# Value products of a fused attention and gated-convolution kernel: two 64-row halves abreast instead of whole 128-row products

## The chip, the cores and the metric

The kernel runs on one core of one Trainium2 chip, in one launch. The metric is the device time of that launch in microseconds, the median of several runs. Beside the times there is one profiled execution, whose trace gives the start and length of every instruction.

## The reference

Eight batches are computed. In each, twelve heads attend over 448 positions with 64 values per head, with a softmax that has one more term in its denominator; the result, 448 x 768, goes through a gated long convolution that is computed by a Fourier transform along the sequence.

```python
scores = scale * np.matmul(q, k.transpose(0, 1, 3, 2))
m = np.max(scores, axis=-1, keepdims=True)
e = np.exp(scores - m)
attn = e / (np.sum(e, axis=-1, keepdims=True) + np.exp(-m) + 1e-09)
...
proj = x @ w_proj
x1, x2, x3 = (proj[..., :D].copy(), proj[..., D:2 * D].copy(), proj[..., 2 * D:].copy())
X2 = np.fft.rfft(x2, n=S, axis=1)
H = np.fft.rfft(filter_fft, n=S, axis=0)[None, :, :]
x2_conv = np.fft.irfft(X2 * H, n=S, axis=1)
y = x1 * x2_conv * x3
return (y @ w_out).astype(np.float32)
```

The change touches only the last product of the attention, `attn @ v`.

## The kernel before

**Attention, pair by pair.** Two heads are worked on together, so there are 8 x 6 = 48 pairs, numbered by `i`. The 448 keys of a head are three blocks of 128 and a remainder of 64. The two remainders of a pair share one block of 128: this is block 0, blocks 1 to 3 are the heads' own keys. `attention(i)` (L859) makes these tasks:

- `scores(t)` (L866): for block 0 one matmul over 128 rows (L873). For blocks 1 to 3 two matmuls (L871), one per head, each over 64 rows (a head has 64 values): head 0 lies on rows 0 to 63 of the array, head 1 on rows 64 to 127, and each writes its own PSUM bank. The two run abreast.
- `exps(t)` (L875): ScalarE's exponentials, from PSUM into the tile `e` (or `er` for block 0), keys on partitions, 448 queries of each head along the row.
- `out_rests` (L898, matmul at L902): the value product of the two remainders. Eight matmuls of 64 rows, 65 columns wide (64 values and a column of ones, which sums the denominator), head 0 on rows 0 to 63, head 1 on rows 64 to 127, each into its head's own bank. The first one of a head opens its sum (`start=True`).
- `out_rest(u)` (L907, matmul at L910): the value product of the own keys of head `u`. Twelve matmuls: four blocks of 128 queries by three blocks of 128 keys, each over all 128 rows, all into head `u`'s bank. There are two such tasks per pair, 96 in all; the text calls them the first and the second value task.
- `norm` (L918): VectorE divides by the denominator once both value tasks are done.

**Dense part.** `dense(b)` (L1027) does projection, transform, gate and output of batch b: matmuls over 128, 113 or 112 rows, 384 to 456 columns wide (L1083, L1105, L1154, L1206, L1253, L1019). A batch's dense part is mixed with the attention of later batches. Near the start, gaps of TensorE that the plan foresees are filled with matmuls on a zero tile (L1501).

**What sets the order.** The kernel is a list of tasks (`add`, L83): engine, cost, what a task needs and makes, what it takes and gives back, and for TensorE the `rows` of the array that it uses (128 unless it is said). `Plan.run` (L92) goes through them at build time and writes out each engine's instructions in a fixed order; with `plan.ORDER` given (L435) an engine's tasks stand in the order of the numbers in that tuple, one number per task, 2135 of them. The plan reckons 0.093 us (`SWITCH`, L66) each time that TensorE's `rows` change from one task to the next. On the chip every engine takes its instructions in that order and waits on semaphores.

**SyncE** (SP) issues nearly all DMAs: loads of q, k and v (L496, L501, L662, L683, L513, L648), transposes by DMA of q, k, of the attention's result and of the transform's input (L632, L639, L977, L1122), and stores (L1339, L1342): 250 in this run. An issue takes SP's time, a transposing one more, and an issue whose data or room is not ready holds up everything behind it. GpSimd converts the loaded q, k and v to bfloat16.

The lines that the change replaces:

```python
def out_rest(u):
    for n in range(NST):
        for t in (0, 2, 1):
            nc.tensor.matmul(
                out_bank(u)[:, n, :],
                P["e"][1 + t][:, u * S + n * 128 : u * S + n * 128 + 128],
                vn[b % 2][:, hp, 4 * u + t, :],
                start=False, stop=(n == NST - 1 and t == 1),
            )
```

Of the kernel before, what the change touches and what calls it, by code (L numbers as in the profile page):

```python
# [18 lines left out]
B, H, S, DH = 8, 12, 448, 64  # L19
D = H * DH  # L20
SP = 112
NST = S // SP
NDT = D // 128
NHP = H // 2
# [17 lines left out]
class Plan:  # L42
# [40 lines left out]
    def add(self, eng, cost, want, emit, need=(), make=(), take=(), give=(), dma=0.0, run=256, n=1, after=0.0, begun=(), late=0.0, turn=False, part=None, keep=False, port=False, rows=128):  # L83
        want = self.ORDER[len(self.tasks)] if self.ORDER else want + self.SHIFT.get(part, 0.0)
        if eng == "SP":
            dma *= self.STRETCH
        if eng == "DVE" and port:
            cost += self.SHARED
        cost, dma, run, late = self.TIMES.get(len(self.tasks), (cost, dma, run, late))
        self.tasks.append((want, len(self.tasks), eng, cost, emit, need, make, take, give, dma, after, run, n, begun, late, turn, keep, port or eng == "POOL" and not dma, rows))  # L90
# [227 lines left out]
def kernel(  # L318
# [11 lines left out]
    nc = tc.nc  # L330
# [69 lines left out]
    vn = [const.tile([128, NHP, 7, DH + 1], BF16, name=f"vn{i}") for i in range(2)]  # L400
# [22 lines left out]
    def stage(g, at, n):  # L423
# [4 lines left out]
    plan = Plan(  # L428
        {
            "e": 6, "er": 2, "e3": 3, "er3": 1, "k0": 2, "q0": 2, "u": 1, "w": 1, "xf": 1,  # L430
            "x2": 1, "x2s": 1, "x2b": 2, "xs": 2, "t0": 2, "t1": 2, "yh": 1, "g": 1, "x1": 2, "cr": 2, "cw": 1, "cv": 2, "yT": 1, "yR": 1,
            "os": 3,
        }
    )
# [3 lines left out]
    add = plan.add  # L438
# [23 lines left out]
    def tau(i, frac=0.0):  # L462

        if i >= NHP * n_batches:
            return tau(i - 1, frac + 1)
        h = i % NHP + frac
        return ATT[i // NHP] + SLOT[i // NHP] * min(h, 3) + LATER[i // NHP] * max(h - 3, 0)
# [391 lines left out]
    def attention(i):  # L859
# [15 lines left out]
        def exps(t):  # L875
            if t:
                P["e"][t] = e = third[t] if i in THIRD else es[(3 * turn_of(i) + t - 1) % 6]
                to, of = e[:, 0 : 2 * S], pair(("sc", ("S", i, t)))[:, :, 0:S]
                if b < NSTAGED:
                    to = to.rearrange("p (u n) -> p u n", u=2)  # L880
                else:
                    to = to.rearrange("p (u n j) -> p u n j", u=2, j=NST)
                    of = of.rearrange("p u (j n) -> p u n j", j=NST)
                nc.scalar.activation(to, of, AF.Exp, scale=SCALE)  # L884
            else:
                P["e"][t] = e = third[0] if i in THIRD else er[turn_of(i) % 2]
                to, of = e[:, 0:S], bank(("hy", ("S", i, t)))[:, 0:S]
                if b >= NSTAGED:
                    to, of = to.rearrange("p (n j) -> p n j", j=NST), of.rearrange("p (j n) -> p n j", j=NST)
                nc.scalar.activation(to, of, AF.Exp, scale=SCALE)  # L890

        def out_banks():
            return pair(("op", i))[:, :, 0 : NST * (DH + 1)].rearrange("p u (n d) -> p u n d", n=NST)

        def out_bank(u):
            return out_banks()[:, u]

        def out_rests():  # L898
            for n in range(NST):
                for u in range(2):  # L900
                    c = slice(64 * u, 64 * u + 64)
                    nc.tensor.matmul(  # L902
                        out_bank(u)[:, n, :], P["e"][0][c, n * 128 : n * 128 + 128], vn[b % 2][c, hp, 3, :],
# [3 lines left out]
        def out_rest(u):  # L907
            for n in range(NST):
                for t in (0, 2, 1):
                    nc.tensor.matmul(  # L910
                        out_bank(u)[:, n, :],
                        P["e"][1 + t][:, u * S + n * 128 : u * S + n * 128 + 128],
                        vn[b % 2][:, hp, 4 * u + t, :],
                        start=False,
                        stop=(n == NST - 1 and t == 1),
                    )
# [41 lines left out]
        for u in range(2):  # L958
            add("PE", 0.37, w + 0.01 * u, lambda u=u: out_rest(u), need=[("ER", i)], make=[("V", i, u)],
                take=[("op", i)], give=[(third_of[0], (i, t)) for t in range(1, 4)])  # L960
# [521 lines left out]
    with (  # L1482
        tc.tile_pool(name="tabs", bufs=1) as tp,
        tc.manual_schedule(engines={E.PE, E.Pool, E.DVE, E.Activation, E.SP}),
    ):
        zero1 = tp.tile([128, 1], F32, name="zero1")
        warm = tp.tile([128, 1], F32, name="warm")
        add("DVE", 0.1, -20.0, lambda: nc.vector.memset(zero1, 0.0), make=["zero1"])
        add("POOL", 0.36, -20.0, count, make=["count"])
        add("POOL", 0.51, -19.0, lambda: make_identity(nc, ident_bf), make=["ident"])  # L1490
        first = tp.tile([1, 16], BF16, name="first")
        add("POOL", 0.64, -18.5, lambda: nc.gpsimd.dma_start(first, moe_w_out[0:1, 0:16]), need=["ident"], dma=0.05)
        add("DVE", 0.2, -19.5, number, need=["count"], make=["row"])
        add("DVE", 2.3, -19.0, phases, need=["row"], make=["phases"])

        idle = tp.tile([128, 128], BF16, name="idle")
        add("DVE", 0.15, -19.9, lambda: nc.vector.memset(idle, 0.0), make=["idle"])

        def fill(i, count):
            for _ in range(count):  # L1500
                nc.tensor.matmul(psum[:, 512 * i : 512 * i + 128], idle, idle)  # L1501

        plan.fill = fill

        def spin():

            t = bank(("hy", "spin"))
            for _ in range(SPIN):
                nc.tensor.matmul(t[:, 0:128], idle, idle)

        add("PE", 3.65, -20.0, spin, need=["idle"], make=["spin"], take=[("hy", "spin")], give=[("hy", "spin")])
        add("ACT", 0.8, -18.0, lambda: nc.scalar.copy(ks, idle[:, None, :].to_broadcast([128, NHP, 128])), need=["idle"], make=["zero ks"])

        add("ACT", 1.3, -20.0, lambda: nc.scalar.activation(warm, zero1, AF.Sin), need=["zero1"], make=["sine table"])
        add("ACT", 0.6, -19.0, sines, need=["phases", "sine table"], make=["sines"])
        add("ACT", 1.5, -16.0, lambda: nc.scalar.activation(warm, zero1, AF.Exp), need=["zero1", "sines"], make=["exp table"])

        def pads():
            for e in es:
                nc.gpsimd.memset(e[:, 2 * S :], 0.0)  # L1520
            for e in er:
                nc.gpsimd.memset(e[:, S:], 0.0)
            nc.gpsimd.memset(third[3][:, 2 * S :], 0.0)

        add("POOL", 0.8, 7.0, pads, make=["pads"], after=6.5)

        def ones(i):
            nc.gpsimd.memset(vn[i][:, :, :, DH : DH + 1], 1.0)
        for i in range(2):
            add("POOL", 0.08, (6.0, 24.0)[i], lambda i=i: ones(i), make=[("ones", i)],  # L1530
                after=(6.5, 16.0)[i])
        for b in range(n_batches):
            if b < NSTAGED:
                staged(b)
            else:
                loaded(b)
        add("DVE", 0.5, tau(NHP * NSTAGED) - 30.0, lambda: nc.vector.memset(kn[:, :, 0, :], 0.0),
            need=[("c" + x, g) for x in "kqv" for g in range(NHP * NSTAGED - NHP, NHP * NSTAGED - 2)], make=["zero kn"])
        for (part, ch), at in zip(LOADS, LOAD):
            if part == "F":  # L1540
                add("POOL", 1.79, at, filter_load, need=["ft", "bps"], make=["filt"], take=[("yT", "F")], dma=3.6, run=115, n=3, late=0.76, after=at)
            elif part == "O":
                add("POOL", 0.82, at, wout_load, make=["wout"], need=[("V", THIRD[-1], 0), ("V", THIRD[-1], 1)], dma=5.95, run=115, late=-0.34, after=at)
            elif ch is None:
                add("POOL", 0.82, at, lambda part=part: wproj_load(part, None), make=[("w", part, 0), ("w", part, 1)], dma=4.9,
                    run=115, late=-0.34, after=at)
            else:
                add("POOL", 0.82, at, lambda part=part, ch=ch: wproj_load(part, ch), make=[("w", part, ch)], dma=2.95, run=55, late=-0.34 if ch else 1.2, after=at)
        more_tables()
        filter_spectrum()  # L1550
        for i in range(n_batches * NHP):
            attention(i)
        for b in range(n_batches):
            dense(b)
        watch()
        tc.mark_branch_hint_location("overflow", 0, engines=[E.PE, E.DVE])
        plan.run()
# [55 lines left out]
```

## Time and profile before

| | |
|---|---|
| time, median of 3 runs | 368.22 us (367.34 to 368.5) |
| profiled execution, first to last instruction | 365.4 us |
| TensorE busy | 358.2 us, 3628 matmuls |
| VectorE, ScalarE, GpSimd busy | 261.7, 263.4, 114.0 us |
| granted TensorE clock | 1.000 throughout |
| DMA | 69.20 MB, mean 189 GB/s |

The profiled execution's span is 2.8 us shorter than the median time; what lies around the span is not in the trace. In the rows below, a group of instructions is shown with its line, engine, operation, what it writes and reads, the shape of the weights and of the moving data, its count, its busy time and the mean length of one. A matmul's length is from its start to its modelled end, so that lengths overlap; the pace is read from the starts. PEld is the weight load that goes with each matmul. SPq is SyncE's queue.

### The profile page before, as it was taken

What the parts mean: (1) busy time and instruction counts of PE and PEld (TensorE: products, weight loads), DVE (VectorE), ACT (ScalarE), POOL (GpSimd) and SP (SyncE); (2) the same over time, 40 slices, a digit from 0 to 9 for tenths busy, and PEclk for the clock granted to TensorE, in tenths of its full rate; (3) what the DMA queues carried; (4) which work ended last, traced back from release to release, by engine and by line L of the source; (5) the groups of instructions that cost most, each with busy time, mean ns of one, the idle gap of its engine ahead of it and who ended that gap; (6) DMA issues with size and microseconds to landing.
All of it is one profiled execution on the core that took longest, in us unless ns stands there. A gap on an engine that the chain in (4) does not pass through costs nothing. (4 is left out here: it accounts for less than half of the span.)

```text
span 365.4 us, 9379 instructions
## 1 busy us (share of the span) xinstructions
PE 358.2 (98%) x3628; PEld 213.2 (58%) x3629; DVE 261.7 (72%) x671; ACT 263.4 (72%) x453; POOL 114.0 (31%) x247
## 2 busy tenths in 40 slices
PE   7999999999999999999999999999999999999995
PEld 6777665656664555655565555654555556555653
DVE  5669299877899549785777758893677867759570
ACT  6989777778796668875777667888877885465433
POOL 7872363315333454345324442700110000000000
PEclk9999999999999999999999999999999999999999
DMA  8999989999999999999999999999942165035025
GB/s 204 270 253 240 248 170 230 230 207 216 157 251 268 249 225 247 200 268 229 260 215 224 309 206 210 210 226 189 219 108 43 45 88 131 0 88 130 26 110 175
DMA packets 135299, 69.20 MB, mean 189 GB/s; under 512 B 91917, under 2 KB 131664, under 8 KB 135248
## 3 DMA queue, kind: packets, MB, share of 16 engines
q1 hardware_dynamic: 130528, 62.90, 78.4%
q0 software_dynamic: 4480, 5.41, 8.8%
q8 instruction: 29, 0.48, 0.6%
q10 hardware_dynamic: 240, 0.23, 0.2%
q14 instruction: 22, 0.18, 0.2%
HBM read 43.86 MB, written 11.01 MB: 150 GB/s over the span
## 5 line engine op out<-in xcount | busy, mean ns | idle before, releaser
L884 ACT ACTIVATE e<-psum 128x896 bf16<-128x896 f32 x138 | 123.0, 922 | 28.8 <-PE psum L871 23.7
L1206 PE MATMUL psum<-xT,wproj_bf 128*128 128x448 bf16 x576 | 121.7, 352 | 0.2 <-DMA xT<-xb 0.2
L1206 PEld LDWEIGHTS <-wproj_bf 128*128 128x128 bf16 x576 | 53.9, 98 | 46.6 <-issue 3.4
L1019 PE MATMUL psum<-wout_bf,yT 128*128 128x384 bf16 (+2 forms) x287 | 54.1, 326 | 0.2
L1105 PE MATMUL psum<-xf,wproj_bf 128*128 128x456 bf16 x216 | 45.7, 356 | 0.0
L910 PE MATMUL psum<-vn,e 128*128 128x65 bf16 x1104 | 45.1, 194 | 0.0
L910 PEld LDWEIGHTS <-e 128*128 128x128 bf16 x1104 | 39.8, 98 | 8.9 <-issue 4.5
L871 PE MATMUL psum<-qT,kT 64*128 64x448 bf16 x288 | 41.9, 354 | 0.2 <-DMA kT<-nat 0.2
L1172 DVE TENSOR_TENSOR t<-xs,hrs 113x768 bf16<-113x768 bf16 (+1 forms) x64 | 39.1, 631 | 3.0 <-ACT xs L1166 2.8
L1222 DVE TENSOR_TENSOR g<-x,psum 128x448 bf16<-128x448 bf16 x42 | 26.0, 618 | 19.0 <-PE psum L1206 16.2
L1332 ACT COPY osb<-psum 128x384 f32<-128x384 f32 (+2 forms) x56 | 26.0, 485 | 17.7 <-PE psum L1019 13.1
L668 POOL CAST nat<-nat 112x512 bf16<-112x512 f32 x36 | 24.3, 679 | 44.1 <-DMA nat<-in_q_dram 44.1
L1166 ACT CAST xs<-psum 113x384 bf16<-113x384 f32 (+1 forms) x64 | 29.1, 484 | 12.3 <-PE psum L1154 8.4
L1019 PEld LDWEIGHTS <-yT 128*128 128x128 bf16 x288 | 27.1, 98 | 18.5 <-issue 1.2
L925 DVE TENSOR_TENSOR xb<-psum,den 128x512 bf16<-128x512 f32 x48 | 33.2, 691 | 1.7
L1220 ACT CAST x<-psum 128x448 bf16<-128x448 f32 x42 | 22.4, 539 | 13.3 <-PE psum L1206 11.7
L700 POOL CAST vn<-nat 128x192 bf16<-128x192 f32 x58 | 21.7, 406 | 32.9 <-DMA nat<-in_v_dram 31.0
L1262 ACT CAST cr<-psum 128x452 bf16<-128x452 f32 x48 | 24.5, 544 | 10.1 <-PE psum L1253 9.2
L1105 PEld LDWEIGHTS <-wproj_bf 128*128 128x128 bf16 x216 | 20.1, 98 | 19.7 <-issue 2.4
L890 ACT ACTIVATE er<-psum 128x448 bf16<-128x448 f32 x46 | 25.4, 555 | 6.9 <-PE psum L873 6.2
L688 POOL CAST nat<-nat 128x384 bf16<-128x384 f32 x29 | 17.6, 612 | 26.6 <-DMA nat<-in_k_dram 24.7
L923 DVE TENSOR_SCALAR den<-psum 128x8 f32<-128x8 f32 x48 | 7.9, 164 | 23.9 <-PE psum L910 23.3
(138 smaller groups left out, 482.0 us busy)
## 6 DMA issues: line engine op xcount, KB each, us to landing
nat<-in_q_dram SPq DMA_DIRECT2D x47, 224.0 KB, 4.6
out_dram<-osb SPq DMA_DIRECT2D x23, 384.0 KB, 3.7
nat<-in_k_dram SPq DMA_DIRECT2D x41, 192.0 KB, 4.7
nat<-in_v_dram SPq DMA_DIRECT2D x41, 192.0 KB, 3.9
wproj_bf<-in_moe_w_proj_dram POOLq DMA_DIRECT2D x2, 1152.0 KB, 12.7
rests<-in_k_dram SPq DMA_DIRECT2D x8, 192.0 KB, 5.0
rests<-in_v_dram SPq DMA_DIRECT2D x8, 192.0 KB, 4.7
out_dram<-osb SPq DMA_DIRECT2D x8, 192.0 KB, 3.2
```

Of the source, the lines that this page charges most:

```text
L871: nc.tensor.matmul(sc[:, u, 0:S], kT[b % 2][c, hp, t, :], qT[b % 2][c, hp, :])
L884: nc.scalar.activation(to, of, AF.Exp, scale=SCALE)
L890: nc.scalar.activation(to, of, AF.Exp, scale=SCALE)
L910: nc.tensor.matmul(out_bank(u)[:, n, :], P["e"][1 + t][:, u * S + n * 128 : u * S + n * 128 + 128], vn[b % 2][:, hp, 4 * u + t, :], start= ...
L925: nc.vector.tensor_tensor(W["xb", b][:, hp].rearrange("p n (u d) -> p u n d", u=2), op[:, :, :, 0:DH], rec[:].unsqueeze(3).to_broadcast([1 ...
L1019: nc.tensor.matmul(ops[:n, : c.stop - c.start], y[:, dt, 0:n], wout_bf[:, dt, c], start=(dt == 0), stop=(dt == NDT - 1),)
L1105: nc.tensor.matmul(pps, wproj_bf[:, kt, D + dt * 128 : D + (dt + 1) * 128], W["xf", b][:, kt], start=(kt == 0), stop=(kt == NDT - 1),)
L1166: nc.scalar.copy(L["xs", par, ch][:K, pg % 2, :], L["Z", pg, ch][:K, :DCH])
L1172: nc.vector.tensor_tensor(t[:K], L["xs", par, ch][:K], h, op=ALU.mult)
L1206: nc.tensor.matmul(p[:, :S], wproj_bf[:, kt, 2 * part * D + dt * 128 : 2 * part * D + (dt + 1) * 128], xT()[:, kt, 0:S], start=(kt == 0), ...
L1222: nc.vector.tensor_tensor(g[:, dt, :], L["x1", dt], p[:, :S], op=ALU.mult)
L1332: (nc.vector.tensor_copy if half else nc.scalar.copy)(L["os", st][:n, c.start + lo : c.start + hi], L["O", st, ch][:n, lo:hi])
```

## The change

A value task no longer belongs to one head. Both tasks of a pair work on both heads, with matmuls of 64 rows: the first task (`s = 0`) multiplies the first 64 keys of each block of head 0 (rows 0 to 63) and the last 64 keys of each block of head 1 (rows 64 to 127), alternating; the second (`s = 1`) the halves that are left, crosswise: head 1 on rows 0 to 63, head 0 on rows 64 to 127. So within a task each head's bank is written from one half of the rows, and between the tasks the two banks change hands. A task has 24 matmuls where it had 12.

Between the two tasks stands a no-operation on SyncE: it waits for the last matmul of the first task, and the first matmul of the second task waits for it. In the list of tasks it is a task of SP of its own, which needs `("va", i)` from the first value task and makes `("vb", i)` for the second; there are 48. Costs: 0.38 for a value task (0.37 before), 0.18 for the no-operation; both value tasks are now marked `rows=64`. `plan.ORDER` is another tuple, with 48 numbers more; `plan.TIMES` is as before.

```diff
-    plan.ORDER = (3, 0, 1, 124, 1, 2, 0, 0, 1, 2, 3, 4, 2, 4, 18, 0, ...)
+    plan.ORDER = (2, 0, 4, 52, 3, 4, 0, 0, 2, 1, 3, 4, 2, 1, 5, 0, ...)
...
+        def follow(ins, other):
+            if other is not None:
+                tc.add_manual_dep(
+                    ins.ins,
+                    other.ins.name,
+                    mybir.DependencyInfo(mybir.DependencyClass.Sync, mybir.DependencyReason.DATA),
+                    reason="the rows of two banks change hands",
+                )
...
-        def out_rest(u):
+        def out_rest(s):
             for n in range(NST):
                 for t in (0, 2, 1):
-                    nc.tensor.matmul(
-                        out_bank(u)[:, n, :],
-                        P["e"][1 + t][:, u * S + n * 128 : u * S + n * 128 + 128],
-                        vn[b % 2][:, hp, 4 * u + t, :],
-                        start=False,
-                        stop=(n == NST - 1 and t == 1),
-                    )
+                    for half in range(2):
+                        u, c = half ^ s, slice(64 * half, 64 * half + 64)
+                        ins = nc.tensor.matmul(
+                            out_bank(u)[:, n, :],
+                            P["e"][1 + t][c, u * S + n * 128 : u * S + n * 128 + 128],
+                            vn[b % 2][c, hp, 4 * u + t, :],
+                            start=False,
+                            stop=(s == 1 and n == NST - 1 and t == 1),
+                        )
+                        if not (n or t or half):
+                            follow(ins, P["swap"] if s else None)
+            if not s:
+                P["swap"] = ins
+
+        def swap():
+            ins = nc.sync.nop()
+            follow(ins, P["swap"])
+            P["swap"] = ins
+
+        P["hand over"] = swap
...
         for u in range(2):
-            add("PE", 0.37, w + 0.01 * u, lambda u=u: out_rest(u), need=[("ER", i)], make=[("V", i, u)],
-                take=[("op", i)], give=[(third_of[0], (i, t)) for t in range(1, 4)])
+            add("PE", 0.38, w + 0.01 * u, lambda u=u: out_rest(u), need=[("vb", i) if u else ("ER", i)], make=[("V", i, u)] + ([] if u else [("va", i)]),
+                take=[("op", i)], give=[(third_of[0], (i, t)) for t in range(1, 4)], rows=64)
...
+        for i in range(n_batches * NHP):
+            add("SP", 0.18, tau(i + 1), T[i]["hand over"], need=[("va", i)], make=[("vb", i)])
```

2 lines of the change are left out of this document (1 added, 1 removed).

## The prediction

> **What bounds the kernel.** I read the page first, then the busy time by stretches, then the order of time on TensorE and on SyncE, then the end of the chain of waits. From the page, the span and TensorE with its clock:
>
> ```profile
> span 365.4 us, 9379 instructions
> PE 358.2 (98%) x3628; PEld 213.2 (58%) x3629; DVE 261.7 (72%) x671; ACT 263.4 (72%) x453; POOL 114.0 (31%) x247
> PEclk9999999999999999999999999999999999999999
> ```
>
> The stretches (columns: busy us and count of PE, PEld, DVE, ACT, POOL; granted clock; share of the DMA engines; GB/s), and the matmuls that fill foreseen gaps:
>
> ```profile
> 5.00:46.00 41.00, 39.59 (x541) 27.72 (x539) 24.99 (x71) 34.01 (x56) 23.45 (x50) 1.00 1.14 254
> 46.00:106.00 60.00, 59.51 (x670) 37.91 (x667) 52.70 (x124) 46.90 (x78) 26.52 (x55) 1.00 1.05 205
> 165.00:265.00 100.00, 99.83 (x980) 55.98 (x979) 70.34 (x177) 74.74 (x130) 34.51 (x68) 1.00 1.09 227
> 265.00:310.00 45.00, 45.00 (x489) 26.14 (x488) 32.82 (x92) 33.26 (x56) 1.75 (x4) 1.00 0.39 82
> ```
>
> ```profile
> L1501 PE MATMUL psum<-idle x101: 217/219/294, 4.7 to 35.0; 128*128 128x128 bf16 x101
> ```
>
> From 46 to 310 us TensorE has work all the time, at full clock; nobody else comes near. So there the time is the sum of TensorE's paces, and what shortens it shortens the kernel. Up to 35 us it is otherwise: 101 filling matmuls stand where TensorE waits for loads. The DMA engines are loaded (share at or over 1) until 265 us.
>
> A busy row hides what a matmul costs; the starts show it (start us, us until the last one's end, what, count):
>
> ```profile
> 13.88 0.90 PE L910 MATMUL psum<-vn,e 128*128 128x65 bf16 x24
> ...
> 45.66 0.91 PE L910 MATMUL psum<-vn,e 128*128 128x65 bf16 x24
> ...
> 199.77 1.30 PE L1206 MATMUL psum<-xT,wproj_bf 128*128 128x448 bf16 x6
> 201.00 0.30 PE L902 MATMUL psum<-vn,er 64*128 64x65 bf16 x8
> 201.13 0.55 PE L871 MATMUL psum<-qT,kT 64*128 64x448 bf16 x4
> 201.61 1.31 PE L1206 MATMUL psum<-xT,wproj_bf 128*128 128x448 bf16 x6
> 202.76 0.53 PE L910 MATMUL psum<-vn,e 128*128 128x65 bf16 x12
> 203.12 2.47 PE L1105 MATMUL psum<-xf,wproj_bf 128*128 128x456 bf16 x12
> 205.43 0.35 PE L873 MATMUL psum<-qT,kT 128*128 128x448 bf16 x1
> ...
> 207.24 0.74 PE L871 MATMUL psum<-qT,kT 64*128 64x448 bf16 x6
> 207.91 2.48 PE L1105 MATMUL psum<-xf,wproj_bf 128*128 128x456 bf16 x12
> 210.33 0.30 PE L902 MATMUL psum<-vn,er 64*128 64x65 bf16 x8
> 210.46 0.35 PE L871 MATMUL psum<-qT,kT 64*128 64x448 bf16 x2
> 210.75 0.91 PE L910 MATMUL psum<-vn,e 128*128 128x65 bf16 x24
> ...
> 301.43 0.54 PE L910 MATMUL psum<-vn,e 128*128 128x65 bf16 x12
> ```
>
> Six L1206 matmuls take 1.15 us to the next start when a 128-row product follows (201.61 to 202.76) and 1.23 when a 64-row one does (199.77 to 201.00). Twelve L1105 take 2.31 before a 128-row product and 2.42 before a 64-row one. Two, four and six scores of 64 rows take 0.29, 0.48 and 0.67 until a 128-row product starts: 0.19 per abreast pair and 0.10 besides. So each change between 64 and 128 rows costs 0.08, 0.11 and 0.10: 0.097 us on the mean.
>
> **Changes of rows: the gain.** I sorted TensorE's 712 tasks by the numbers of the old and of the new tuple, with the rows that each task names, and counted neighbours whose rows differ: 164 before, 124 after. The new tuple gathers a pair into blocks such as remainder product, scores, first value task, two scores, second value task, all of 64 rows. With the old tuple and new rows it would be 222: the order, not the halving, makes the gain. Up to the last pair's second value task 41 are saved (one comes back at the end): 15 up to that of pair 6 (the row at 45.66), 26 after it. 26 x 0.097 = 2.5 us, on TensorE's path, where nothing covers it. The 15 early ones, 1.5 us, lie where TensorE waits for loads; they are worth from 0, if all becomes waiting, to 1.5. I take half, 0.7.
>
> **The value matmuls themselves.** Twice as many, half as high:
>
> ```profile
> L910 PE MATMUL psum<-vn,e 128*128 128x65 bf16 x1104 | 45.1, 194 | 0.0
> L902 PE MATMUL psum<-vn,er 64*128 64x65 bf16 x368 | 13.3, 191 | 0.1
> ```
>
> The new form is that of L902 at three times the length. L902's 368 stand in 46 groups of eight, 13.3 / 46 = 0.289 us each; less the last one's own 0.191, four pairs start within 0.098, so a pair takes about 0.031. Twelve whole products last 0.53 (202.76), less 0.194, over eleven steps: 0.0305 each. A task of twelve pairs against twelve whole ones thus costs 0 to 0.01 us more, 96 tasks 0 to 1.0; I take 0.5. No row shows 24 in one run; a shortage of weight loads or of issue would show there, and is a rival below. The sentence of the Trainium skill that speaks against this part is on its page "TensorE: Matmul & The Clock Gate", section "Wait — 56ns, not 53.3ns?": matmuls never start less than about 25 ns apart, however narrow; 24 in a task would then take an estimated 0.60 us, and the 96 tasks some 22 us more than now. The trace disagrees where 64-row halves alternate: eight in 0.13 us (201.00 to 201.13), 16 ns apart.
>
> **The hop over SyncE.** It goes: last matmul of the first task ends, the no-operation wakes and ends, TensorE's second task wakes. The nearest rows are at the end of the chain of waits, and SP's own short instruction at L639:
>
> ```profile
> 356.60 0.04 issue
> 356.64 3.73 PE psum L1019 x21
> ...
> 360.43 1.26 PE psum L1019 x8
> 361.69 0.04 DVEq L1332
> 361.73 0.04 issue
> 361.77 0.30 DVE osb L1332
> ```
>
> ```profile
> L639 SPq DMA_TRANSPOSE kT<-nat x16: 1188/1860/3036, 60.7 to 245.2; - x16
> L639 SPq EVENT_SEMAPHORE  x12: 17/17/282, 60.6 to 233.0; - x12
> ```
>
> 0.19 for the matmul to end, 0.08 from its end into a waiting engine by way of its sequencer (361.69 to 361.77), 0.04 onto TensorE (356.60): 0.31 and the no-operation. Under it lie, by the new tuple, in 33 of 48 pairs exactly two scores of 64 rows, 0.38 to 0.39 us, and the 0.03 until they start: 0.42. The no-operation may take 0.11. I take the semaphore instruction's 17 ns, as it also only waits, so a hop to an idle SP is free; the other end is a DMA issue (0.47 at 203.31 below), 0.36 over, in 48 pairs 17 us. Eight pairs have more work between, four early ones one score only (about 0.1 late each, in the filled stage), three others about as much as the 33.
>
> That holds if SP is already waiting in the no-operation. In the trace of before it mostly would not be:
>
> ```profile
> 13.52 2.21 SPq L496 DMA_DIRECT2D nat<-in_q_dram  x1
> ...
> 203.31 0.47 SPq L683 DMA_DIRECT2D nat<-in_v_dram  x1
> ...
> 301.40 1.28 SPq L1122 DMA_TRANSPOSE x<-nat  x1
> ```
>
> Taking the end of each pair's first value task as the hop's moment, SP is inside a DMA issue at 35 of 48, with 24.1 us left in all, 0.69 each; the first is pair 0, whose twelve matmuls from 13.88 on are done at 14.4, with SP busy until 15.7, the last pair 46, from 301.43 and done at 302.0, with SP busy until 302.7. The new order puts the no-operations between the issues, so that SP should stand ready: it must then finish what is ahead in time. Ahead of 14 no-operations is a transposing DMA (1.19 to 3.04 us at L639), of 5 a store that needs a result copied first, of 4 another no-operation, of 25 a load. A late one holds TensorE, which cannot pass its second value task: 0.69 less the 0.09 that is left of the cover, 0.60 us each. I take one, 0.6 us; both ends are under the rivals. Behind a waiting no-operation stand the next loads, transposes and stores; GpSimd's conversions wait for those, then the scores. Loads lie well ahead of their use in the steady part, so I price this at nothing there; without that lead it is a rival.
>
> **Elsewhere.** VectorE's division still follows the second value task. 1152 more matmuls and loads cost only the pace counted above. The new tuple moves other tasks too; TensorE's idle time to be had or lost outside the changes is small in the stretches above (0.49 us of 60, 0.17 of 100), and I put it at 0.
>
> **Sum.** -2.5 - 0.7 + 0.5 + 0.6 = -2.1 us: span 363.3 for 365.4. The median stands 2.8 us over the span, and I let that stay: 368.2 - 2.1 = 366.1.
>
> **Rivals.**
>
> *The hops give the gain back* (no change). Without a late hop the sum is -2.7. Three to six late ones leave -0.9 to +0.9: 367.3 to 369.1. For it: an SP that would be busy at 35 of 48 moments, and transposes of scattered length. Against: between two hops SP has some 6 us and about five issues (250 issues, 48 pairs in 290 us), and a wait for TensorE sets it right again. Loads held behind waiting no-operations, with the DMA engines at a share over 1, would do the same.
>
> *SyncE's issues become the bound* (slower). The same wait, at seven hops or more: from +1.5 us on. In the part up to 265 us a transpose that takes 3.0 us instead of 1.2 makes every later no-operation late until SP catches up. Seven to fourteen late hops give 369.7 to 373.9; all 35 would be +18, 386. Against: SP may stand waiting most of the time.
>
> *Halves don't run abreast when 24 follow each other* (slower). If each takes a whole product's 0.0305, a task takes 0.73 for 0.37, 96 tasks +35 us: 403. Eight at 16 ns speak against it. (The page's floor of 25 ns, above, is the milder form, some +22 by the estimate there.)
>
> *The early changes* are inside the forecast: early changes worth 0 and two late hops give -2.5 + 0.5 + 1.2 = -0.8, about 367.4; all worth 1.5, no dearer matmuls and no late hop -4.0, 364.2.
>
> **How the numbers follow.** Forecast 0.52 (364.2 to 367.1, as far as it is faster), gain given back 0.23, SyncE the bound 0.23, halves in turn 0.02. A measurement here tells 0.3%, 1.1 us, from no change. The range goes from 364.2 up to nine late hops, -2.7 + 5.4, rounded to 371.0; left out are the upper part of SyncE's case, 0.12, halves in turn, and a little below. Faster 0.52, same 0.23, slower 0.25.
>
> **What would show it.** The value matmuls as 2304 of 64x65, with about 0.37 us from the start of a task to the next start; about 40 fewer steps of 0.097. If 0.4 us or less lies between first and second value task, the hop is free; a second task starting after an idle TensorE, with SP's no-operation starting late behind a DMA issue, is the second or third case. A no-operation over 0.11 us with SP idle before it, or a task of over 0.45 us, would prove me wrong; so would filling matmuls or early idle time that grow by what the early changes save.

## The result, and the profile after

The changed kernel takes 384.85 us, the median of 4 runs (380.91 to 386.59); the kernel before took 368.05 us (4 runs, 367.34 to 368.5). The ratio is 1.0435, with a 95% interval of 1.0376 to 1.0494: slower, where 366.1 us and at most 371.0 had been forecast. The profiled execution is the fastest of the four, 380.91 us with a span of 379.0; the last section says what that hides. In the experiments below, two executions (389.08 and 386.61 us) fell in a slower state of the chip and do not count in the ratios; without them the medians of their kernels are 382.35 and 381.33 us.

The page of after: the span, the engines, and TensorE's clock in 40 slices.

```profile
span 379.0 us, 11681 instructions
PE 357.4 (94%) x4744; PEld 216.8 (57%) x4745; DVE 254.2 (67%) x671; ACT 262.4 (69%) x452; POOL 108.8 (29%) x247
PEclk9999998999999999999999999999999999999999
```

TensorE is busy for 0.8 us less than before, and the span is 13.6 us longer. It stands idle instead. Where it does is seen in the stretches that the prediction shows of before, and in 106 to 165 us, whose row of before follows (busy us and count of PE, PEld, DVE, ACT, POOL; granted clock; share of the DMA engines; GB/s):

```profile
5.00:46.00 41.00, 37.41 (x630) 25.99 (x629) 25.19 (x72) 33.85 (x55) 21.89 (x47) 1.00 1.15 241
46.00:106.00 60.00, 54.58 (x851) 35.95 (x851) 42.22 (x110) 41.00 (x69) 21.48 (x48) 0.97 0.99 193
106.00:165.00 59.00, 56.78 (x756) 31.80 (x754) 39.28 (x99) 43.34 (x75) 24.02 (x53) 1.00 1.04 231
165.00:265.00 100.00, 98.04 (x1313) 56.92 (x1312) 71.96 (x186) 73.44 (x126) 32.97 (x70) 1.00 0.98 222
265.00:310.00 45.00, 44.79 (x686) 26.76 (x685) 30.90 (x83) 36.83 (x62) 4.47 (x9) 1.00 0.47 99
```

Before, from 106 to 165 us:

```profile
106.00:165.00 59.00, 58.84 (x604) 32.30 (x602) 44.69 (x111) 44.95 (x77) 23.85 (x51) 1.00 1.12 245
```

From 46 to 106 us TensorE idles for 5.42 us (0.49 before), from 106 to 165 for 2.22 (0.16 before), from 165 to 265 for 1.96 (0.17 before), and from 5 to 46 for 3.59 (1.41 before). From 265 us on, where the share of the DMA engines is down at 0.47, it idles for 0.21 us of 45.

The groups of TensorE's matmuls, with what ended the idle time before them (busy us, mean ns of one | idle us before and releaser):

```profile
L1041 PE MATMUL psum<-wout_bf,yT 128*128 128x384 bf16 (+2 forms) x287 | 54.3, 326 | 2.6 <-ACTq L1585 1.9 <-ACT osb L1354 0.6
L921 PE MATMUL psum<-vn,e 64*128 64x65 bf16 x2208 | 49.3, 191 | 7.7 <-SPq L934 7.6
L911 PE MATMUL psum<-vn,er 64*128 64x65 bf16 x368 | 13.3, 191 | 1.9 <-POOL vn L556 1.7 <-ACT e L884 0.2
```

L921 is the value matmul and L934 the no-operation. Read by itself this points at the hop, 7.6 us of it, in 9 waits. That reading turns out to be wrong as an answer to where the time went, and the experiments below are about it.

The steady part looks as foretold. The order of time on TensorE (start us, us until the last one's end, what, count):

```profile
208.53 0.28 PE L911 MATMUL psum<-vn,er 64*128 64x65 bf16 x8
208.65 0.53 PE L921 MATMUL psum<-vn,e 64*128 64x65 bf16 x24
209.02 0.54 PE L871 MATMUL psum<-qT,kT 64*128 64x448 bf16 x4
209.40 0.53 PE L921 MATMUL psum<-vn,e 64*128 64x65 bf16 x24
209.86 1.31 PE L1228 MATMUL psum<-xT,wproj_bf 128*128 128x448 bf16 x6
```

24 halves take 0.37 us until the scores start, the second task follows 0.38 us later behind two pairs of scores, and the hop costs nothing. The no-operation is a semaphore instruction of 17 ns:

```profile
L934 SPq EVENT_SEMAPHORE  x48: 17/17/17, 12.5 to 315.8; - x48
```

It goes otherwise at 57 us. SyncE's and TensorE's order of time there:

```profile
50.93 0.63 SPq L501 DMA_DIRECT2D nat<-in_v_dram  x1
59.78 0.98 SPq L683 DMA_DIRECT2D nat<-in_k_dram  x2
```

```profile
57.16 0.53 PE L921 MATMUL psum<-vn,e 64*128 64x65 bf16 x24
60.26 0.95 PE L921 MATMUL psum<-vn,e 64*128 64x65 bf16 x30 [2.56 <-SPq L934]
```

The load of v issued at 50.93 lands at 59.0; SyncE stands until then at the next load, which waits for it, and the no-operation of the waiting pair comes after that, at 60.2. TensorE idles for 2.56 us. Of the 48 no-operations 16 start more than 0.15 us after their first value task is done, 1.2 us on the mean; 12 of them lie between 57 and 200 us, where the share of the DMA engines is about 1.

### The profile page after: what moved, and what is told of

It reads as the page before. It is cut to its first block, busy times and chain, and to the rows that moved or that the text cites. A ratio compares the mean times of both kernels' runs of the same rounds, so it can differ in the third digit from the quotient of the medians.

```text
span 379.0 us, 11681 instructions
## 1 busy us (share of the span) xinstructions
PE 357.4 (94%) x4744; PEld 216.8 (57%) x4745; DVE 254.2 (67%) x671; ACT 262.4 (69%) x452; POOL 108.8 (29%) x247
## 5 line engine op out<-in xcount | busy, mean ns | idle before, releaser
L884 ACT ACTIVATE e<-psum 128x896 bf16<-128x896 f32 x138 | 121.3, 922 | 23.2 <-PE psum L871 19.3
L1228 PEld LDWEIGHTS <-wproj_bf 128*128 128x128 bf16 x576 | 54.8, 98 | 48.1 <-issue 3.2
L1041 PE MATMUL psum<-wout_bf,yT 128*128 128x384 bf16 (+2 forms) x287 | 54.3, 326 | 2.6 <-ACTq L1585 1.9
L921 PE MATMUL psum<-vn,e 64*128 64x65 bf16 x2208 | 49.3, 191 | 7.7 <-SPq L934 7.6
L921 PEld LDWEIGHTS <-e 64*128 64x128 bf16 x2208 | 41.8, 95 | 17.3 <-SPq L934 15.0
L871 PE MATMUL psum<-qT,kT 64*128 64x448 bf16 x288 | 42.9, 352 | 1.2 <-DMA qT<-nat 0.4
L1194 DVE TENSOR_TENSOR t<-xs,hrs 113x768 bf16<-113x768 bf16 (+1 forms) x64 | 36.8, 592 | 7.2 <-ACT xs L1188 7.1
L1041 PEld LDWEIGHTS <-yT 128*128 128x128 bf16 x288 | 27.0, 98 | 21.1 <-issue 3.2
L668 POOL CAST nat<-nat 112x512 bf16<-112x512 f32 x36 | 23.4, 654 | 43.9 <-DMA nat<-in_q_dram 42.7
L1242 ACT CAST x<-psum 128x448 bf16<-128x448 f32 x42 | 22.6, 543 | 15.1 <-PE psum L1228 14.9
L1127 PEld LDWEIGHTS <-wproj_bf 128*128 128x128 bf16 x216 | 20.5, 98 | 18.5 <-issue 0.4
L688 POOL CAST nat<-nat 128x384 bf16<-128x384 f32 x29 | 15.1, 530 | 30.0 <-DMA nat<-in_k_dram 29.9
## 6 DMA issues: line engine op xcount, KB each, us to landing
wproj_bf<-in_moe_w_proj_dram POOLq DMA_DIRECT2D x2, 1152.0 KB, 11.5
```

The source lines that it names most:

```text
L871: nc.tensor.matmul(sc[:, u, 0:S], kT[b % 2][c, hp, t, :], qT[b % 2][c, hp, :])
L921: ins = nc.tensor.matmul(out_bank(u)[:, n, :], P["e"][1 + t][c, u * S + n * 128 : u * S + n * 128 + 128], vn[b % 2][c, hp, 4 * u + t, :], ...
L1041: nc.tensor.matmul(ops[:n, : c.stop - c.start], y[:, dt, 0:n], wout_bf[:, dt, c], start=(dt == 0), stop=(dt == NDT - 1),)
L1127: nc.tensor.matmul(pps, wproj_bf[:, kt, D + dt * 128 : D + (dt + 1) * 128], W["xf", b][:, kt], start=(kt == 0), stop=(kt == NDT - 1),)
L1194: nc.vector.tensor_tensor(t[:K], L["xs", par, ch][:K], h, op=ALU.mult)
L1228: nc.tensor.matmul(p[:, :S], wproj_bf[:, kt, 2 * part * D + dt * 128 : 2 * part * D + (dt + 1) * 128], xT()[:, kt, 0:S], start=(kt == 0), ...
```

## The experiments

Each run is compared with the kernel before on the same chip; in brackets stands the 95% interval of the ratio. The theories of the first four runs: **A**, the hop over SyncE and SyncE's late no-operations are the cause (as the third case of the prediction has it); **B**, the newly laid order is slow by itself, with or without crossing; **C**, 24 halves cost more than 12 whole products.

**The new order without crossing.** The halves stay on their rows (head 0 on 0 to 63, head 1 on 64 to 127) in both tasks, and the no-operation goes; half of the keys are counted twice and the other half left out.

```diff
-                        u, c = half ^ s, slice(64 * half, 64 * half + 64)
+                        u, c = half, slice(64 * half, 64 * half + 64)
...
-            ins = nc.sync.nop()
-            follow(ins, P["swap"])
```

> The changed kernel with its order, its halves and its plan, but both value tasks of a pair take the same halves (head 0 always rows 0 to 63, head 1 always rows 64 to 127), so no bank changes hands and there is neither a no-operation nor a wait for one. It leaves out the last 64 keys of head 0's blocks and the first 64 of head 1's and counts the others twice; its matmuls are as many and as large as the changed kernel's. Theory A, SyncE comes late to the no-operations and the no-operations hold its loads back: all of the loss goes, and 40 changes of rows fewer than before remain: 364.5 to 367. Rival B, the new order is bad by itself, the hop only shows where it waits: 376 or more. Rival C, the halves cost more than whole products: near the changed kernel, 380 or more.

Measured: 381.89 us (379.9 to 383.06), ratio 1.0399 [1.0365, 1.0433]. A falls as the main cause: with no hop at all, nearly the whole loss is still there.

**The new order with whole products.** `out_rest` as before the change, 128 rows, no no-operation; 210 changes of rows in the plan, for 124 in the run above.

```diff
-                    for half in range(2):
-                        u, c = half ^ s, slice(64 * half, 64 * half + 64)
+                    nc.tensor.matmul(out_bank(u)[:, n, :], P["e"][1 + t][:, ...], vn[b % 2][:, hp, 4 * u + t, :], ...)
```

> The new order with the value products of before (whole, 128 rows, one head to a task), no no-operations and no waits for them. The new order then has 210 changes of rows, before 164: 46 more at 0.097 us. Theory A: 368.05 + 4.5, about 372.5 (371 to 374). Rival B, the order is bad by itself: 380 or more. Rival C, the halves cost: about 368 to 372 as well; the run without crossing tells A from C.

Measured: 382.8 us (380.38 to 389.08), ratio 1.0413 [1.0372, 1.0454]. As B says; C falls, since no halves are left in it. But there is a riddle: by the plan it has 86 more changes of rows than the run above, by the traces 80 (214 for 134, filling matmuls included), some 8 us by the price of 0.097, and it is only 0.9 us slower (0.5 by the ratios, with an uncertainty of about 2).

**Whole products, with the no-operations and their waits.**

```diff
+                    if not (n or t):
+                        follow(ins, P["swap"] if u else None)
```

> The new order with the value products of before, but with the no-operations kept: each waits for a pair's first value task, and the second waits for it. Nothing of the halves is in it. Theory A: the hop's loss is there without the halves, and the changes of rows too: the changed kernel's 384.85 and up to 8.3 us (86 changes more) on it, 384 to 393. Rival B: the same as without no-operations, 380 or more for both. Rival C: much less than the changed kernel, 372 to 376.

Measured: 384.89 us (383.0 to 385.76), ratio 1.0467 [1.0419, 1.0515]. By the medians the hops cost 2.1 us here and 3.0 between the changed kernel and the run without crossing, by the ratios 2.0 and 1.3; in both pairs the intervals overlap, so that anything from 0 to about 4 us is what these four kernels tell of it.

**The old order with halves that don't cross.** This is the kernel before, order and plan untouched, with another `out_rest`.

```diff
-        def out_rest(u):
+        def out_rest(s):
...
+                    for u in range(2):
+                        c = slice(64 * u, 64 * u + 64)
```

> The kernel before with its own order, plan and costs, but with the halves abreast, uncrossed and without no-operations, as in the run without crossing (same keys left out). In the old order the 64-row value tasks give 222 changes of rows for 164. Theory A with the prices of the prediction: 58 x 0.097 = 5.6 and 0 to 1.0 for the matmuls: 373.7 to 374.7. Rival C, a task of 24 halves takes 0.1 us longer than one of 12 whole products: 383 or more. If changes of rows cost nothing: 368 to 369.

Measured: 377.06 us (376.63 to 378.2), ratio 1.0263 [1.0227, 1.0298], 9.6 us above before. The trace has 230 changes of rows for 172 (filling and turning matmuls included): 58 x 0.097 = 5.6 us. That is 2 to 3 us more than theory A foretold; three waits in the first 36 us that before does not have (1.15, 0.98 and 0.80 us) make up most of it. Halves in the old order lose, as the prediction said; but the old order with 230 changes is still faster than the new one with 134.

**Which engine's new order?** With whole products throughout, the numbers of the new tuple were given to some engines only. If the transfers stand wrongly (theory **T**) the new numbers of SyncE and GpSimd should lose alone; if the compute engines do (theory **C**, another one than above) those of TensorE, VectorE and ScalarE; if the five are laid for one another (theory **M**) both mixtures should be bad.

```diff
-    plan.ORDER = (3, 0, 1, 124, 1, 2, ...
+    plan.ORDER = (new number for each task of SyncE and GpSimd, old number for the others)
```

> Whole value products, no no-operation; SyncE's and GpSimd's own tasks stand in the new order, TensorE's, VectorE's and ScalarE's in the old one (so the changes of rows stay at 164). The new order with whole products took 382.8 us and 210 changes of rows; 46 of those at 0.097 us are 4.5 us, and 10.3 us are left for the order itself. Theory T (the new order of the transfers lets loads and transposes arrive after TensorE's turn): 376 to 380 us. Theory C (the new order of the compute engines asks for things before they can come): 367 to 370 us. Theory M (the five orders are laid for one another, and a mixture loses more than either): 380 us or more here and in the mirrored mixture.

Measured: 401.48 us (398.52 to 402.57), ratio 1.0907 [1.0854, 1.096].

> The mirror of the first: whole value products, no no-operation; TensorE's, VectorE's and ScalarE's tasks in the new order (210 changes of rows, 4.5 us above before), SyncE's and GpSimd's in the old one. Theory T: 371 to 374 us, the changes of rows alone. Theory C: 380 to 384 us, as with all five orders new. Theory M: 380 us or more here and in the first.

Measured: 398.84 us (394.89 to 399.85), ratio 1.0835 [1.0783, 1.0886]. M holds: no engine's new order is the bad one by itself. What TensorE waits for in the first mixture and in the second (the groups with the longest waits for transfers, as above):

```profile
L873 PE MATMUL psum<-qT,kT 128*128 128x448 bf16 x48 | 17.6, 367 | 5.8 <-DMA kT<-nat 4.9 <-DMA qT<-nat 0.9
L1154 PE MATMUL psum<-x,ft 113*113 113x384 bf16 (+1 forms) x48 | 14.8, 349 | 8.4 <-DMA x<-xb 8.4
```

```profile
L1154 PE MATMUL psum<-x,ft 113*113 113x384 bf16 (+1 forms) x48 | 14.6, 346 | 13.0 <-DMA x<-xb 5.3 <-DMA x<-nat 3.7 <-DVE g L1222 2.4
```

In these groups it is a transfer that ends most of the idle time, whichever side was moved. Over all of TensorE's matmuls, transfers end 14.5 of 21.4 us of idle time in the first mixture and 9.0 of 20.1 in the second, for 0.3 of 3.1 in before.

**Which part of the span?** All five engines in the new order for the tasks that the plan begins in the first 50 us, in the old one from there; and the mirror.

```diff
-    plan.ORDER = (3, 0, 1, 124, 1, 2, ...
+    plan.ORDER = (new number for each task of the first 50 us, old numbers behind them)
```

> Whole value products, no no-operation; all five engines in the new order for the tasks of about the first 50 us, in the old order from there (168 changes of rows, 0.4 us above before). If the order loses at the start, where the records of the new order fall 4 to 7 us behind before by the sixth to twelfth pair: 371 to 375 us. If it loses evenly over the span: 1.4 us of order and 0.4 us of changes, 369 to 370.5 us.

Measured: 370.14 us (10 runs, 369.59 to 371.51), ratio 1.0044 [1.0022, 1.0066].

> The mirror of the third: the old order for about the first 50 us, the new one from there (206 changes of rows, 4.1 us above before). If the order loses at the start: 374 to 378 us. If evenly: 380 to 382 us.

Measured: 382.11 us (378.53 to 386.61), ratio 1.0312 [1.0242, 1.0383]. Most of the loss comes with the part after 50 us; the new order of the first 50 us alone costs 1.5 us.

**Transfers, taken at their word.** What TensorE waits for in the run without crossing, where no hop hides it:

```profile
L1226 PE MATMUL psum<-xT,wproj_bf 128*128 128x448 bf16 x576 | 123.2, 356 | 3.8 <-DMA wproj_bf<-in_moe_w_proj_dram 2.2 <-DMA xT<-xb 1.5
L1039 PE MATMUL psum<-wout_bf,yT 128*128 128x384 bf16 (+2 forms) x288 | 54.4, 326 | 2.5 <-ACTq L1583 1.8 <-ACT osb L1352 0.6
L871 PE MATMUL psum<-qT,kT 64*128 64x448 bf16 x288 | 43.1, 352 | 2.4 <-DMA kT<-nat 1.6 <-ACT kT L579 0.3 <-ACT er L890 0.2
L1174 PE MATMUL psum<-x,ft 113*113 113x384 bf16 (+1 forms) x48 | 13.5, 332 | 2.3 <-DMA x<-xb 2.2
```

The first and the third of these groups in before:

```profile
L1206 PE MATMUL psum<-xT,wproj_bf 128*128 128x448 bf16 x576 | 121.7, 352 | 0.2 <-DMA xT<-xb 0.2
L871 PE MATMUL psum<-qT,kT 64*128 64x448 bf16 x288 | 41.9, 354 | 0.2 <-DMA kT<-nat 0.2
```

In all, transfers end 8.3 of TensorE's 15.6 us of idle time here. So a last theory, **Q**: the DMA engines have no room (a share at or near 1 until 265 us), and the new order lets TensorE ask for what has not landed. Its rival, **E**: the engines wait for one another's work, however fast the transfers are. Both are tried by making the transfers lighter and nothing else: from the second use of each staging room on, a load of q, k or v brings one head's half of it, and the other half keeps older numbers.

```diff
-    nc.sync.dma_start(src.rearrange("p (u c) -> p u c", u=2), rows(x, b, hp))
+    nc.sync.dma_start(src.rearrange("p (u c) -> p u c", u=2)[:, 0 : 2 if b * NHP + hp < 15 else 1], rows(x, b, hp)[:, 0 : 2 if b * NHP + hp < 15 else 1])
```

> The kernel before, but from the fifth pair on in the first two batches and from the second round of the staging rooms on in the others, each load of q, k and v brings one of its two heads only (the other head's half of the room keeps older numbers); about 12 of the 69 MB that the DMA engines move are left out, and no instruction. Theory Q (the transfer queues, 9 tenths busy up to 270 us, have no room, and the new order makes TensorE ask for what has not landed): this order waits 0.4 us for DMA in all, so 366 to 368.5 us. The rival, theory E (the new order makes the engines wait for one another's work, whatever the transfers): the same, 366 to 368.5 us.

Measured: 367.25 us (366.34 to 370.51), ratio 0.9985 [0.9956, 1.0013]. The kernel before gains nothing that can be measured from a load that is lighter by 13 of 69 MB.

> The new order with halves abreast that don't cross, no no-operation (as the first run of the study, 381.9 us), with the same half of the loads left out. Its TensorE has 21.6 us of gaps of over 60 ns above the usual pitch, before has 4.1 us. Theory Q: most of the 17.5 us between them goes, but not the 2.4 us at the end where no loads run; 367 to 373 us. Theory E: 379 us or more.

Measured: 370.67 us (367.65 to 371.96), ratio 1.0048 [1.0017, 1.0079]. The same new order gains 11.2 us from it. E falls as the main cause: what holds the engines goes, for the most part, when nothing but the transfers is changed. Not all of it goes, and that much is left open below. Idle time of TensorE that transfers end goes from 8.3 to 3.5 us, and all its idle time from 15.6 to 9.8. Of the groups above, the fourth goes from 2.3 to 0.5 us of idle time, the first from 3.8 to 0.4; the third, the scores, does not gain. The first and the third with light loads (each line number is one higher here):

```profile
L1227 PE MATMUL psum<-xT,wproj_bf 128*128 128x448 bf16 x576 | 121.5, 353 | 0.4 <-DMA wproj_bf<-in_moe_w_proj_dram 0.2
L872 PE MATMUL psum<-qT,kT 64*128 64x448 bf16 x288 | 43.1, 352 | 3.3 <-DMA kT<-nat 1.2
```

The stretches, where the idle time of TensorE from 5 to 265 us is 6.6 us, for 13.0 with all loads:

```profile
5.00:46.00 41.00, 38.59 (x691) 27.09 (x692) 27.12 (x75) 35.03 (x58) 26.08 (x53) 1.00 1.01 203
46.00:106.00 60.00, 58.26 (x884) 37.37 (x883) 47.52 (x120) 45.31 (x76) 23.80 (x50) 1.00 0.84 169
106.00:165.00 59.00, 57.84 (x818) 33.38 (x817) 42.09 (x110) 43.42 (x74) 23.28 (x48) 1.00 0.94 192
165.00:265.00 100.00, 98.72 (x1317) 57.84 (x1316) 70.97 (x175) 75.17 (x129) 33.00 (x69) 1.00 0.80 170
```

The same of the run without crossing and with all loads:

```profile
5.00:46.00 41.00, 36.39 (x602) 24.33 (x601) 24.40 (x69) 31.30 (x49) 22.08 (x47) 0.96 1.16 249
46.00:106.00 60.00, 56.61 (x883) 37.47 (x881) 44.40 (x113) 43.76 (x76) 21.48 (x47) 1.00 0.96 187
106.00:165.00 59.00, 56.98 (x760) 32.33 (x759) 40.45 (x101) 44.32 (x76) 26.01 (x54) 1.00 1.06 232
165.00:265.00 100.00, 97.04 (x1308) 56.75 (x1307) 72.86 (x183) 72.44 (x124) 32.78 (x71) 1.00 1.02 222
```

Lightening does two things at once. The share of the DMA engines falls (0.96 to 1.16 in these stretches with all loads, 0.80 to 1.01 with light ones), and each load lands sooner: a load of k took 4.3 us from issue to landing without crossing (median) and 3.0 with half of the data, one of v 4.7 and 3.4. Which of the two gives the order its room isn't separated. With all loads a landing takes about as long in before, 4.7 for k and 3.9 for v. That points at when the loads are issued and asked for, and not at slower transfers.

> The changed kernel itself (crossed, with its 48 no-operations on SyncE), with the same half of the loads left out; it took 384.9 us with all of them. Theory Q: SyncE stands less long at landings, so the late no-operations get fewer too; 369 to 375 us. Theory E: 381 us or more. The hop's own price is the difference to the run without crossing: 3 us if SyncE's lateness has nothing to do with loads, under 1.5 us if it has.

Measured: 370.52 us (369.66 to 372.92), ratio 1.0065 [1.0036, 1.0093], beside the run without crossing on the same chip: the 48 hops cost nothing that can be measured here (0.6 us by the ratios, with an uncertainty of 1.5). They still come late at times:

```profile
PEld L922 <- SPq L935: 9.0, 28, 1.9
```

This row of the waits view of after with light loads (L922 the value matmul, L935 the no-operation; us, times, longest) reads 15.1 us, 32 times, with all loads. So late starts at the hop seem to be made good elsewhere: what TensorE would have waited for next is there when it comes. That is a reading of the times; no run shows it wait by wait.

**Where the saving of the changes of rows went.** The riddle of the first two runs, tried again with room in the transfers: new order, whole products, light loads.

> The new order with whole value products of 128 rows (no crossing, no no-operation), with the same half of the loads left out. Against the run with halves and light loads (370.7 us) it differs in the rows alone: 210 changes in the plan for 124, 86 at 0.097 us are 8.3 us. With all loads this difference gave 0.9 us (382.8 for 381.9). If the saving of the changes is real and was given back to late transfers (theory Q): 376 to 379 us. If a change of rows on the path costs little in this order: 370 to 373 us.

Measured: 377.73 us (376.01 to 379.85), ratio 1.0252 [1.0178, 1.0326]. Against halves with light loads that is 7.1 us by the medians, 7.5 by the ratios (another chip; the uncertainty is 3), for 8.3 foretold; with all loads it was 0.9. A change of rows has its price, and with all loads the saving is given back: a TensorE that is quicker comes to the next transfer earlier and waits there. The traces with all loads bear this out. The halves without crossing have 15.6 us of idle time, 8.3 of it ended by transfers, and the whole products 11.5 and 4.5.

## Why the prediction was wrong

**The step that failed** is the one under "Elsewhere": "The new tuple moves other tasks too; TensorE's idle time to be had or lost outside the changes is small in the stretches above (0.49 us of 60, 0.17 of 100), and I put it at 0." Those rows bound what a new order can win from TensorE's idle time. They say nothing of what it can lose. The loss was 14.5 us in the run without a hop, and with the loads lightened 11.2 us of it went: the new order makes TensorE wait for transfers that the old one found landed. The row to read was in the same stretches: a share of the DMA engines of 1.05 to 1.14 until 265 us. Both mixtures of the two orders were slower than either whole one, 398.84 and 401.48 us: the orders of the engines are laid for one another. That the old one was fitted to when things land is the likely reading, not a measurement. "The new tuple moves other tasks too" was most of the change, and should have had a rival of its own, with a price that has no end at 0.

**Changes of rows** (-2.5 and -0.7): counted nearly rightly, 172 to 134 in the traces with all matmuls. The price fits: 7.1 to 7.5 us for the 80 changes between the two traces are about 0.09 each, though the uncertainty of 3 us would allow 0.06 to 0.13. What it is worth with all loads was wrong: 0.9 us for 80. "On TensorE's path, where nothing covers it" holds only where the next transfer is early enough.

**The value matmuls** (+0.5): from the first to the last start of a task the median is 0.343 us, for 0.340 before, and the 96 tasks sum to 33.6 us for 32.7: +0.9, inside the 0 to 1.0. Two tasks of 0.54 and 0.61 us, at 60.3 and 60.9 us under half the clock (see the last section), make up 0.5 of it. The Trainium skill's page "TensorE: Matmul & The Clock Gate", section "Wait — 56ns, not 53.3ns?", states that starts are never less than about 25 ns apart; 24 starts in 0.343 us are 15 ns apart, so for halves that alternate between row groups the measurement decides against it.

**The hop** (+0.6, one late): free to a SyncE that waits, as reckoned, and a no-operation takes the 17 ns that were assumed. That "SP should stand ready" was wrong for 16 hops, 12 of them from 57 to 200 us, each 1.2 us late on the mean where 0.69 was reckoned; this is the place of the third case of the prediction, and its mechanism is real, at 57 us with 2.56 us of idle time. It was not what decided: the new order without it was 14 us slower than before, and the hops' own share, loads held behind them included, is 0 to about 4 us.

**The count** of TensorE's time, from the start of each matmul: over the usual pitch of its form and of a change of rows, gaps of more than 60 ns sum to 22.1 us, for 4.1 before: +18.0. The 38 fewer changes give -3.7, 36 fewer filling matmuls at 0.056 us -2.0, the value tasks +0.9. That is +13.2, and the last matmul starts and ends 12.8 us later; from there to the end of the span it is 4.6 us for 3.7.

**What stays open.** With light loads the new order is still 3.4 us behind before with light loads, though it has 38 fewer changes, 3.7 us by the price of 0.097. So some 7 us of the order's own loss are left, of some 18 with all loads (14.5 and 3.7), and their cause isn't shown. Of the 9.8 us of idle time that TensorE has there, transfers still end 3.5 and VectorE 3.1. 2 us of the loss lie at the end, where TensorE waits in every run of the whole new order for ScalarE, which stands at the kernel's last branch (1.9 us at L1041 above); why it gets there late wasn't tried. Which of the many moved loads and transposes are the costly ones wasn't separated either. A crossing without the hop wasn't tried.

## What to carry to other kernels

An order of instructions that was fitted to one set of arrival times is itself part of the speed: price a re-laid order as a change of its own, with a loss that is not bounded by today's idle time. Loaded DMA engines that cost nothing today (lightening them gained before 0.7 us, inside its uncertainty) can cost a new order much (11.2 us here), and can make savings on the bounding engine vanish (0.9 us left of some 8). To learn whether late transfers are the cause, lighten the transfers in both kernels and leave every instruction in its place; the waits view alone named the no-operation, with 7.6 us, and leaving it out gained 0 to 4.

## What the runs showed of the hardware beside that

After a long wait of TensorE its granted clock falls to half for 3.41 us. Work that fills such a stretch takes an estimated 1.7 us longer, on top of the wait. Of after (stretch, busy us and count of PE, PEld, DVE, ACT, POOL; clock; share of the DMA engines; GB/s):

```profile
57.60:60.20 2.60, 0.10 (x8) 0.00 (x0) 0.22 (x1) 0.00 (x0) 1.08 (x3) 1.00 1.02 189
60.40:63.80 3.40, 3.40 (x55) 2.25 (x51) 2.50 (x8) 1.24 (x3) 2.80 (x7) 0.50 0.93 169
63.80:68.00 4.20, 4.20 (x26) 1.91 (x25) 4.02 (x10) 2.70 (x5) 0.16 (x1) 1.00 1.13 225
```

In the run without crossing the same follows its wait of 2.22 us at 34.6 (clock 0.51 from 37.0 to 40.4). There is no sharp limit in these traces. All eleven waits of 2.30 us or more within the work were followed by a fall. Between 1.85 and 2.23 us it goes either way: in the new order with whole products a wait of 2.23 us at the same place, 34.4, left the clock at 1.00, as one of 1.93 did with the no-operations, while with whole products and light loads a fall came 2.1 us after a wait of 1.85. The Trainium skill's page "TensorE: Matmul & The Clock Gate", Part 1, has the clock fall after at least one idle window of about 3.4 us; here waits from 1.85 us on sufficed, and the half rate lasted as long as that page's window.

This also makes the profile of after too kind. Its one fall and the end of the span give a mean clock of 0.994; the other three executions have 0.980 to 0.986 over spans of 382.7 to 384.7 us. By the same reckoning that is an estimated three to four falls in each, 5 to 7 us where the profiled execution lost 1.7.
